# Spreading the sequence products to the end of attention, and loading the operands of the output projection ahead of their use

## The chip, the cores and the metric

The kernel runs on one core of a Trainium2 chip. The metric is the device time of one execution in microseconds (us). Engines are named as in the profile: PE is TensorE (its weight loads PEld), DVE VectorE, ACT ScalarE, POOL GpSimd, and SP the engine whose queue issues nearly all DMAs.

## What is computed

```python
x = A_x                                                     # [1, 2048, 512]
g = sigmoid((x * gate_w).sum(-1, keepdims=True))
# part A: real part of a 2-d DFT, as products with cos and sin matrices
a = dft_seq_re @ (x @ dft_hid_re.T) - dft_seq_im @ (x @ dft_hid_im.T)
# part B: causal attention in a window of 256 keys, 32 heads of 16
q, k, v = split(x @ wqkv)
p = softmax(where(0 <= i - j < 256, q @ k.T / 4, -1e9))
b = (p @ v) @ wo
return g * a + (1 - g) * b
```

All tensors are float32. Products that need it are split into a high and a low part (hi, lo), and three products replace one.

## The kernel before

**Two kinds of work on TensorE.** The attention runs in a main loop written out over n, and all other products ("dense" ones) come from one generator, `dense()`, from which `fill(n)` takes a number of steps per turn of the loop. A step is one product of hi and lo parts; in the loop it is written as two matmuls of 64 rows each. `fill` is called twice for each of the four turns p of a block n, and adds `rate / 2` to a quota each time; each whole quota is one step. The order of instructions on each engine is that in which this Python code issues them. A small clock (`tick`) counts steps, and `defer(ticks, fn)` puts a later instruction at the place where the clock has gone on by so many ticks. So `defer` sets places in the lists of the engines, not times.

**Attention.** 128 blocks (8 groups of 4 heads by 16 blocks of 128 rows). The S products of block n (`s_head`, L417) give row maxima by a fused step on DVE (L420). Four blocks of maxima are negated, split (L427, L428), transposed (L430), written to `m_scr` by DMA and read back into two rows of the tile `ring0`, as mask rows of the T products. Nine blocks later (`LAG`) the T products of block k = n - 9 (`t_head`, L472) are made, ACT takes their exponential (L473) into a tile `pt`, and POOL masks two parts of it (`t_mask`, L479 and L483). After every four blocks P V follows (`pv`, L498), 48 matmuls; ACT copies one half (L504), DVE adds the other (L505), and the result goes to DRAM (`u_scr`) and is repacked by DMA into `o_scr` (the values) and `l_scr` (the sums). The sums are read, inverted on DVE (L527) and written back.

The last nine turns of the loop have no S any more: these are the T blocks 119 to 127, with three P V between and behind them.

**Sequence products.** After the projections ("proj"), `c_block` makes 16 blocks of the DFT along the sequence, 24 steps each (L246). Each is evicted by ACT and DVE (L749 to L756), mixed into its rows (L765 to L774) and stored in `r_scr[tb]`. The last pair of blocks, 13 and 3, is mixed together, after the second of them. In this stage `rate` is the constant `FILL_SEQ = 2.3`. When the last block has been issued, "seq" is set.

**Output projection.** For each quarter `sb` of the rows and each of four groups g, `o_load` loads the broadcast inverse sums (`rl`) and the values (`o`), DVE multiplies them (L854), ACT casts the product to its high part in two pieces (L102), and DVE makes the low part in two (L105). The operands of quarter 0 are prepared as soon as its sums are there, those of 1 and 2 not before "seq", those of 3 after attention. Then `wo_run` makes tile tb = 0 to 15 with 12 products each (L242), and DVE adds the gated product to the mixed row read back from `r_scr` (L893), which is stored in `out`. Before tile 0 the first three mixed rows are read into the tile `fin`, which lies where `ring0` was.

The lines that the change touches are `FILL_SEQ` and `fill`, the count in `c_block`, `attention_done`, `o_load`, `wo_get`, `wo_run`, and the loop.

Of the kernel before, what the change touches and what calls it, by code (L numbers as in the profile page):

```python
# [18 lines left out]
D = 512  # L19
# [7 lines left out]
SCALE = 0.25  # L27
LAG = 9
NPT = 7
FILL_FIRST, FILL_PROJ, FILL_SEQ = 4.0, 1.55, 2.3  # L30
TERMS = ((0, 0), (0, 1), (1, 0))
HALVES = slice(0, 512), slice(512, 1024)
H = D // 2 + 1
# [18 lines left out]
def fnet_window_mix(ctx: ExitStack, tc: tile.TileContext, xT, x, wqk, wv, wm, wx, cc, wo, gw, out):  # L52
    nc = tc.nc
# [18 lines left out]
    r_scr = [dram.tile([P, D], F32, name=f"r_scr{c}") for c in range(16)]  # L72
# [22 lines left out]
    def ld(dst, src):  # L95
        nc.sync.dma_start(dst, src)  # L96

    def f(ap):
        return ap.bitcast(F32)

    def hi_of(hi, raw):
        nc.scalar.copy(hi, raw)  # L102

    def lo_of(lo, raw, hi, pool=False):
        (nc.gpsimd if pool else nc.vector).tensor_sub(lo, raw, f(hi))  # L105
# [6 lines left out]
    def split_raw(raw, at_=0, step=0, pool=0):  # L112
        t = st.tile([P, 2, 1024], F32R, name="hl")
        hi, lo = t[:, 0], t[:, 1]
        for n, c in enumerate(HALVES):
            for m, (fn, *args) in enumerate(((hi_of, hi[:, c], raw[:, c]), (lo_of, lo[:, c], raw[:, c], hi[:, c], pool > n))):
                if step:
                    defer(at_ + step * (n + 2 * m), fn, *args)
                else:
                    fn(*args)  # L120
        return hi, lo

    def big_tile():
        return big.tile([P, 2, U_W], F32R, name="big")
# [42 lines left out]
    for dk in range(DK):  # L167
        c = slice(dk * 256, dk * 256 + 256)
# [11 lines left out]
    for dk in (1, 2, 3, 0):  # L180
        if dk:
            first_w(dk)
        t = XT[dk, 0]
# [65 lines left out]
    def es_tile():  # L249
        return ev.tile([P, U_W], F32, name="es", bufs=3)  # L250
# [377 lines left out]
        nc.vector.tensor_scalar(flag, gl[0:1, 10:11], 0.0, None, op0=OP.is_le)  # L628

    order = CLEAR + [tb for p in PAIRED for tb in p]  # L630
    MRAW = {}
    MHL = {}

    def main_load(n):
        if n < len(order):
            tb = order[n]
            MRAW[n] = st.tile([P, 1024], F32, name="raw", bufs=3)
            b = MAINS[tb % 4]
            ld(MRAW[n].rearrange("p (q x) -> p q x", q=4),
               cc[tb][:, :, b:b + 2].rearrange("q p i t -> p q (i t)"))  # L640

    def main_split(n, at_=1, step=4):
        if n < len(order):
            MHL[n] = split_raw(MRAW.pop(n), at_, step, 2)

    def c_block(n, done):
        tb = order[n]
        clear = tb % 2 == 0
        pss = acc()
        hl = MHL.pop(n)  # L650
        m = 0
        for i in range(2):
            u = slice(0, H + 1) if i == 0 else slice(H, D + 1) if clear else slice(H + 1, 2 * H + 2)
            o = slice(H - 1, D) if clear and i else slice(0, H + 1)
            for q in range(4):
                k = (2 * q + i) * P
                for x, y in TERMS:
                    mm([ps[:, o] for ps in pss], hl[x][:, k:k + P], U[tb % 4, q][:, y, u], m == 0, m == 23,
                       True)
                    m += 1  # L660
                    if m < 24:
                        yield
        if FIN:
            wo_run()
        done(tb, pss)
        main_split(n + 2)
        defer(10, main_load, n + 3)
        yield

    have = set()  # L670

    def dense():
# [147 lines left out]
    def attention_done():  # L820
        FIN.append(const.tile([P, 8, 512], F32, name="fin", tag="ring0"))
        RL.append(const.tile([P, 4, 2, 512], F32, name="rl", tag="ring1"))
        for tb in range(3):
            defer(1 + 6 * tb, wo_get, tb)

    def by_class(ap):
        return ap.rearrange("r (c p) -> r c p", c=4)

    def rows_of(ap):
        return ap.rearrange("r (p c) -> r c p", c=4)  # L830
# [10 lines left out]
    def o_load(sb, g):  # L841
        ls = l_scr[sb][g // 2]
        if sb == 3:
            t = pt_tile([P, 3, 512], F32R)
            o = f(t[:, 2])
        else:
            t = big_tile()[:, :, 0:512]
            o = f(t[:, 1])
        rl = RL[0][:, sb * 2 - 4 + g // 2, g % 2] if FIN and sb > 1 else es_tile()[:, 0:512]
        ld(rl, bass.AP(tensor=ls.tensor, offset=ls[1, g % 2 * 8].offset, ap=[[512, 8], [0, 16], [1, 512]]))  # L850
        ld(o, o_scr[sb][g])

        def product():
            nc.vector.tensor_mul(rl, o, rl)  # L854
            defer(4, high)

        def high():
            for c, p in TURNS:
                hi_of(by_class(t[:, 0])[:, c], rows_of(rl)[:, c, p])
            defer(4, low)  # L860

        def low():
            for c, p in TURNS:
                lo_of(by_class(t[:, 1])[:, c], rows_of(rl)[:, c, p], by_class(t[:, 0])[:, c])
            defer(8, OHL[sb].append, t)
        defer(16, product)

    def wo_get(tb):
        if tb in stored and tb not in wo_r:
            wo_r[tb] = FIN[0][:, tb % 8]  # L870
            ld(wo_r[tb], r_scr[tb])

    def wo_run():
        nonlocal wo_next
        tb = wo_next
        sb, c = divmod(tb, 4)
        if tb > 15 or len(OHL.get(sb, ())) < NG or len(WO) < 4:
            return tick()
        wo_get(tb)
        if tb not in wo_r:  # L880
            return tick()
        wo_next += 1
        r = wo_r.pop(tb)
        w = 256 if tb == 15 else 512
        for q in range(0, 512, w):
            k = slice(q, q + w)
            ps = ps_a.tile([P, 512], F32, name="t", tag="st")
            n = 0
# [4 lines left out]
            nc.vector.scalar_tensor_tensor(r[:, k], ps[:, :w], g0[:, tb:tb + 1], r[:, k], op0=OP.mult, op1=OP.add)  # L893
            defer(3 if tb == 15 else 8, ld, out[sb][:, c, k], r[:, k])
        wo_get(tb + 3)

    stream = dense()
# [9 lines left out]
    def ring_ahead(n):  # L907
        nonlocal loaded
        while loaded < 4 * NS:
            g, ss = divmod(loaded, 4)  # L910
            if n >= NB * g + 4 * ss:
                need(("qk", g // 2, ss))
            if ("qk", g // 2, ss) not in have or n - LAG < NB * (g - 1) + 4 * ss + 5:
                break
            ring_load(g, ss)
            loaded += 1

    def fill(n):
        nonlocal quota
        rate = FILL_FIRST if n < LAG else FILL_SEQ if "proj" in have else FILL_PROJ  # L920
        quota += rate / 2
        while quota >= 1:
            next(stream, None)
            quota -= 1

    N = NS * NB
# [10 lines left out]

    for n in range(N + LAG + 1):
        k = n - LAG
        ring_ahead(n + 1)  # L940
        if k in (-2, 0):
            v_ahead(k // 2 + 1)
        for p in range(NH):
            if 0 <= k < N > n:
                s_head(n, p)
                t_head(k, p ^ 1)
            elif p % 2 == 0:
                for j in range(p, p + 2):
# [158 lines left out]
```

## Time and profile before

| | us |
|---|---|
| median of three runs | 731.53 |
| lowest and highest | 730.19, 732.51 |
| profiled execution | 732.08 |
| its span | 730.2 |

| engine | busy us in the span |
|---|---|
| PE | 603.6 |
| DVE | 495.2 |
| POOL | 435.1 |
| ACT | 428.4 |

The mean granted clock of TensorE was 0.877 of full speed. A row of the timeline gives the start and duration in us, the engine, the line of the kernel, the operation, and out<-in by the program's names with partitions x elements. Rows of one group in a row are merged (x96). In brackets stands how long the engine sat idle before it, and who released it. "SPq" rows are issues of DMAs. In the chain of waits a row is the start, the duration, and the work that held up the end at that time. A row of a stage gives, for the time from A to B, the stage's length, the busy time of each engine with its number of instructions, the granted clock, the share of the DMA engines and GB/s. Numbers of lines in rows are those of the kernel before; in the changed kernel L854 is L857, and L893 is L896.

### The profile page before, as it was taken

How to read it: one execution, taken by the hardware profiler on the slowest of the kernel's cores; microseconds unless marked ns; L12 is line 12 of the kernel's file. 1: busy time of each engine (PE TensorE's matmuls, PEld its weight loads, DVE VectorE, ACT ScalarE, POOL GpSimd, SP SyncE). 2: the span in 40 equal slices, each digit the busy share in tenths (PEclk: the TensorE clock that was granted, in tenths of full speed). 3: DMA queues.
4: the chain of work that ended last, by engine and by line, in shares of the span. 5: the costliest groups of instructions: out<-in, count | busy, mean ns of one | idle time of the engine just before them, and what ended most of it. 6: DMA issues, size and time to landing. Idle time of an engine off the chain costs nothing. (4 is left out here: it accounts for less than half of the span.)

```text
span 730.2 us, 17617 instructions
## 1 busy us (share of the span) xinstructions
PE 603.6 (83%) x6222; PEld 450.6 (62%) x6222; DVE 495.2 (68%) x1419; ACT 428.4 (59%) x952; POOL 435.1 (60%) x521
## 2 busy tenths in 40 slices
PE   9999699899788898988868887769777799559885
PEld 6788466666454666665546566657666587437664
DVE  5278677787787788787766765675688677344561
ACT  6434578677556676665556767476667668652220
POOL 6012557676687766678584979988988746420000
PEclk9999889999999999889988897667779969858898
DMA  7777677787565778567586699856566743655883
GB/s 278 259 233 199 205 228 225 228 263 210 176 201 172 213 227 273 179 202 207 169 262 214 210 268 278 269 148 188 171 195 197 207 138 117 190 174 145 259 276 110
DMA packets 93605, 152.61 MB, mean 209 GB/s; under 512 B 33028, under 2 KB 42116, under 8 KB 93380
## 3 DMA queue, kind: packets, MB, share of 16 engines
q1 hardware_dynamic: 92068, 149.28, 66.9%
q10 hardware_dynamic: 1440, 2.10, 0.9%
q8 instruction: 53, 0.87, 0.6%
q14 instruction: 44, 0.36, 0.2%
HBM read 108.56 MB, written 47.24 MB: 213 GB/s over the span
## 5 line engine op out<-in xcount | busy, mean ns | idle before, releaser
L420 DVE CUSTOM_DVE_ANT_0 sm<-s,mask 128x384 bf16<-128x384 f32 (+2 forms) x512 | 270.3, 528 | 104.3 <-PE s L417 54.7
L473 ACT ACTIVATE pt<-t 128x384 f32<-128x384 f32 (+2 forms) x512 | 231.4, 474 | 101.1 <-PE t L472 77.8
L472 PE MATMUL t<-ring,ring 50*128 50x384 f32 (+2 forms) x512 | 218.3, 442 | 59.0 <-ACT pt L473 30.1
L246 PE MATMUL d<-big,hl 64*128 64x512 f32 (+2 forms) x1440 | 248.8, 384 | 0.5 <-DVE es L257 0.5
L417 PE MATMUL s<-ring,ring 48*128 48x384 f32 (+2 forms) x512 | 199.0, 400 | 33.0 <-DVE nm L420 28.7
L246 PEld LDWEIGHTS d<-big,hl 64*128 64x128 f32 x1440 | 177.0, 223 | 6.5 <-issue 1.7
L417 PEld LDWEIGHTS s<-ring,ring 48*128 48x128 f32 x512 | 106.2, 212 | 99.6 <-DVE nm L420 86.7
L479 POOL TENSOR_SCALAR_AFFINE_SELECT pt<-pt 128x512 f32<-128x512 f32 x128 | 83.0, 649 | 140.5 <-ACT pt L473 140.0
L472 PEld LDWEIGHTS t<-ring,ring 50*128 50x128 f32 x512 | 108.1, 214 | 91.3 <-ACT pt L473 46.4
L246 PE MATMUL d<-hl,big 64*128 64x512 f32 x600 | 111.7, 416 | 0.0
L498 PE MATMUL o<-pt,vpad 64*32 64x320 f32 (+5 forms) x2816 | 89.2, 392 | 15.9 <-POOL pt L479 10.8
L498 PEld LDWEIGHTS o<-pt,vpad 64*32 64x32 f32 x2816 | 69.1, 117 | 38.4 <-POOL pt L479 13.6
L339 POOL TENSOR_TENSOR cv<-cv 128x256 f32<-128x256 f32 (+1 forms) x64 | 74.4, 1163 | 20.4 <-DMA cv<-cc 16.9
L483 POOL TENSOR_SCALAR_AFFINE_SELECT pt<-pt 128x512 f32<-128x512 f32 x112 | 74.8, 667 | 0.0
L246 PEld LDWEIGHTS d<-hl,big 64*128 64x128 f32 x600 | 67.1, 195 | 4.8 <-issue 1.0
L504 ACT COPY es<-o 128x512 f32<-128x512 f32 x32 | 18.8, 586 | 82.0 <-PE o L498 77.9
L342 POOL TENSOR_TENSOR cv<-cv 128x512 f32<-128x512 f32 x48 | 62.9, 1311 | 0.0
L540 ACT ACTIVATE cv<-cv 128x768 f32<-128x768 f32 x72 | 60.6, 842 | 0.6 <-POOL cv L339 0.6
L505 DVE TENSOR_TENSOR es<-o,es 128x512 f32<-128x512 f32 x32 | 22.0, 688 | 43.2 <-ACT es L504 35.9
L105 POOL TENSOR_TENSOR hl<-es,hl 128x512 fp32r<-128x512 f32 x14 | 18.5, 1319 | 48.0 <-ACT hl L102 48.0
L105 POOL TENSOR_TENSOR hl<-raw,hl 128x512 fp32r<-128x512 f32 x35 | 45.4, 1309 | 2.2 <-ACT hl L102 2.2
L242 PE MATMUL t<-big 128*128 128x512 f32 x144 | 40.0, 438 | 8.1 <-DVE fin L893 8.1
(98 smaller groups left out, 648.3 us busy)
## 6 DMA issues: line engine op xcount, KB each, us to landing
cv<-cc SPq DMA_DIRECT2D x64, 512.0 KB
qk_scr<-hl SPq DMA_DIRECT2D x32, 512.0 KB
ring<-qk_scr SPq DMA_DIRECT2D x128, 128.0 KB
ring<-qk_scr SPq DMA_DIRECT2D x128, 64.0 KB
u_scr<-es SPq DMA_DIRECT2D x32, 256.0 KB
raw<-cc SPq DMA_DIRECT2D x16, 512.0 KB
fin<-r_scr SPq DMA_DIRECT2D x17, 256.0 KB
big<-c_scr SPq DMA_DIRECT2D x16, 258.0 KB
```

The source lines that it names most:

```text
L105: (nc.gpsimd if pool else nc.vector).tensor_sub(lo, raw, f(hi))
L246: nc.tensor.matmul(pss[h], w[r], x[r], start=start, stop=stop, skip_group_check=skip)
L339: (nc.gpsimd if pool else nc.vector).tensor_sub(out, a, b)
L342: (nc.gpsimd if pool else nc.vector).tensor_add(out, a, b)
L417: nc.tensor.matmul(ps[:, :w], ring[0][r, p, jb * P:(jb + 1) * P], ring[1][r, p, k0:k0 + w], start=True, stop=True)
L420: nc.vector.tensor_tensor_reduce(out=sm[:, :w], in0=ps[:, :w], in1=mask[:, WIN - w:], scale=1.0, scalar=3e38, op0=OP.add, op1=OP.min, accu ...
L472: nc.tensor.matmul(ps[:, :w], ring[1][r, p, q0:q0 + P], ring[0][r, p, q0:q0 + w], start=True, stop=True)
L473: nc.scalar.activation(pt[:, j, :w], ps[:, :w], AF.Exp, scale=-1.0)
L479: nc.gpsimd.affine_select(a, a, pattern=[[0, 4], [1, P]], compare_op=OP.is_ge, fill=0.0, base=0, channel_multiplier=-1)
L483: nc.gpsimd.affine_select(a, a, pattern=[[0, 4], [-1, P]], compare_op=OP.is_gt, fill=0.0, base=0, channel_multiplier=1)
L498: nc.tensor.matmul(ot[h][32 * j:32 * j + 32, a - sb * 512:e - sb * 512], v2[r, j], pt[r, j, a - kb * P:e - kb * P], start=kb == kbs[0], st ...
L540: nc.scalar.activation(junk, src, AF.Abs, accum_out=dst)
```

## The change

1. In the stage of sequence products the rate is no longer a constant: it is reckoned at each call so that 48 steps (`SEQ_END`, two blocks) are left when S ends (n = N), and these are spread over the nine turns that have T blocks alone. For this `c_block` counts the steps that are left.
2. In `o_load` the inverse sums of quarters 0 to 2 are loaded into the half of the `big` tile where the high part will stand, instead of into an `es` tile (there are three of those) or the tile `rl`; the product goes to an `es` tile. The product stands 24 ticks behind the loads instead of 16, but for the last quarter.
3. The first three mixed rows are read into the tiles T[0] to T[2], which are free by then, from n = N + 4 on, where they are stored. All other mixed rows are read by DMAs that ACT issues instead of SP.
4. A result is stored 13 ticks after its sum instead of 8 (but for the last), and the masks of a T block without S are placed 1 tick after it instead of 3.

```diff
-FILL_FIRST, FILL_PROJ, FILL_SEQ = 4.0, 1.55, 2.3
+FILL_FIRST, FILL_PROJ, SEQ_END = 4.0, 1.55, 48
...
+                    left[0] -= 1
...
-            defer(1 + 6 * tb, wo_get, tb)
+            wo_get(tb)
...
-        rl = RL[0][:, sb * 2 - 4 + g // 2, g % 2] if FIN and sb > 1 else es_tile()[:, 0:512]
+        rl = RL[0][:, g // 2, g % 2] if sb == 3 else f(t[:, 0])
...
         def product():
-            nc.vector.tensor_mul(rl, o, rl)
-            defer(4, high)
+            to = rl if sb == 3 else es_tile()[:, 0:512]
+            nc.vector.tensor_mul(to, o, rl)
+            defer(4, high, to)
...
-        defer(16, product)
+        defer(16 if sb == 3 else 24, product)
...
         if tb in stored and tb not in wo_r:
-            wo_r[tb] = FIN[0][:, tb % 8]
-            ld(wo_r[tb], r_scr[tb])
+            wo_r[tb] = T[tb][:, 0:D] if tb < 3 else FIN[0][:, tb % 8]
+            (ld if tb < 3 else nc.scalar.dma_start)(wo_r[tb], r_scr[tb])
...
-            defer(3 if tb == 15 else 8, ld, out[sb][:, c, k], r[:, k])
+            defer(3 if tb == 15 else 13, ld, out[sb][:, c, k], r[:, k])
...
-        rate = FILL_FIRST if n < LAG else FILL_SEQ if "proj" in have else FILL_PROJ
+        if n < LAG:
+            rate = FILL_FIRST
+        elif "proj" not in have:
+            rate = FILL_PROJ
+        elif n < N:
+            rate = max(0, left[0] - SEQ_END) / (4 * (N - n) - 2)
+        else:
+            rate = left[0] / (4 * (N + LAG - n) - 2) if n < N + LAG else 0
...
+        if n >= N + 4:
+            for tb in range(3):
+                wo_get(tb)
...
-                defer(3, t_mask, k)
+                defer(3 if n < N else 1, t_mask, k)
```

How this moves instructions is seen at three places. The first is ACT in the T blocks without S, from the first P V there (the first L504) on. Before:

```order
L504 COPY es<-o 128x512
L473 ACTIVATE pt<-t 128x384 x4
L102 CAST big<-es 128x384
L102 CAST big<-es 128x128
L473 ACTIVATE pt<-t 128x384 x2
L102 CAST big<-es 128x384
L102 CAST big<-es 128x128
L473 ACTIVATE pt<-t 128x384 x2
L749 ACTIVATE es<-d_9756 128x258
```

And in the changed kernel:

```order
L504 COPY es<-o 128x512
L473 ACTIVATE pt<-t 128x384 x10
L751 ACTIVATE es<-d_9677 128x258
L473 ACTIVATE pt<-t 128x384 x4
L775 ACTIVATE ev<-es,g_332 128x257
L776 ACTIVATE ev<-es,g_332 128x255
L473 ACTIVATE pt<-t 128x384 x2
L102 CAST big<-es 128x384
L102 CAST big<-es 128x128
L504 COPY es<-o 128x512
```

The first cast of an operand of the output projection (big<-es) stood behind four exponentials, and now stands behind sixteen, just ahead of the copy of the next P V. Before the third P V all eight operands of quarters 0 and 1 were cast, now those of quarter 0 alone.

The second place is SP in the same stage, from the write of the last mask rows (m_scr_162) to their read. Before:

```order
L96 DMA m_scr_162<-mt 4x32x32
L96 DMA u_scr_1_177<-es 128x512
L96 DMA es<-l_scr_0_166 128x1x512
L96 DMA big<-o_scr_182 128x512
L96 DMA vr<-v_scr_113 128x4x64
L96 DMA es<-l_scr_1_167 128x1x512
L96 DMA big<-o_scr_182 128x512
L96 DMA ring_309<-m_scr_162 2x2x384 x2
```

And in the changed kernel:

```order
L96 DMA m_scr_162<-mt 4x32x32
L96 DMA u_scr_1_177<-es 128x512
L96 DMA vr<-v_scr_113 128x4x64
L96 DMA l_scr_1_167<-lt 128x64
L96 DMA big<-l_scr_0_166 128x1x512
L96 DMA big<-o_scr_182 128x512
L96 DMA ring_309<-m_scr_162 2x2x384 x2
```

Between the two there were two pairs of loads of operands (a pair is l_scr and o_scr), and there is one now, with the write of the inverse sums (l_scr<-lt); the load of the sums' broadcast goes to `big` instead of `es`.

The third place is DVE in the output projection, from the sum of a mixed row to the first low parts that follow. Before, at tile 0:

```order
L893 SCALAR_TENSOR_TENSOR fin<-t,g_333,fin 128x512
L854 TENSOR_TENSOR es<-big,es 128x512
L105 TENSOR_TENSOR big<-es,big 128x384
L105 TENSOR_TENSOR big<-es,big 128x128
L854 TENSOR_TENSOR rl<-big,rl 128x512
L893 SCALAR_TENSOR_TENSOR fin<-t,g_333,fin 128x512
```

And in the changed kernel, from tile 1 to tile 3:

```order
L896 SCALAR_TENSOR_TENSOR t_270<-t,g_333,t_270 128x512
L896 SCALAR_TENSOR_TENSOR t_271<-t,g_333,t_271 128x512
L857 TENSOR_TENSOR es<-big 128x512 x2
L527 RECIPROCAL lt<-lt 128x64
L896 SCALAR_TENSOR_TENSOR fin<-t,g_333,fin 128x512
L105 TENSOR_TENSOR big<-es,big 128x384
L105 TENSOR_TENSOR big<-es,big 128x128
L105 TENSOR_TENSOR big<-es,big 128x384
L105 TENSOR_TENSOR big<-es,big 128x128
L857 TENSOR_TENSOR es<-big 128x512 x2
```

Before, the operands that were made beside the first tiles were those of quarter 2; now they are the first of quarters 1 and 2, by turns (x2), and the sum of tile 3 stands ahead of their first low parts. On PE the last step of the sequence products stands behind the third P V, right ahead of the first product of the output projection; before, the last twenty T products and two P V had no step between them.

More of the change, by code (lines that the diff above doesn't have):

```diff
@@ L630, in fnet_window_mix @@
     order = CLEAR + [tb for p in PAIRED for tb in p]
+    left = [16 * 24]
     MRAW = {}
@@ L853, in product, with high, low @@
         def product():
-            nc.vector.tensor_mul(rl, o, rl)
-            defer(4, high)
-        def high():
+            to = rl if sb == 3 else es_tile()[:, 0:512]
+            nc.vector.tensor_mul(to, o, rl)
+            defer(4, high, to)
+        def high(o):
             for c, p in TURNS:
-                hi_of(by_class(t[:, 0])[:, c], rows_of(rl)[:, c, p])
-            defer(4, low)
-        def low():
+                hi_of(by_class(t[:, 0])[:, c], rows_of(o)[:, c, p])
+            defer(4, low, o)
+        def low(o):
             for c, p in TURNS:
-                lo_of(by_class(t[:, 1])[:, c], rows_of(rl)[:, c, p], by_class(t[:, 0])[:, c])
+                lo_of(by_class(t[:, 1])[:, c], rows_of(o)[:, c, p], by_class(t[:, 0])[:, c])
             defer(8, OHL[sb].append, t)
-        defer(16, product)
+        defer(16 if sb == 3 else 24, product)
     def wo_get(tb):
         if tb in stored and tb not in wo_r:
-            wo_r[tb] = FIN[0][:, tb % 8]
-            ld(wo_r[tb], r_scr[tb])
+            wo_r[tb] = T[tb][:, 0:D] if tb < 3 else FIN[0][:, tb % 8]
+            (ld if tb < 3 else nc.scalar.dma_start)(wo_r[tb], r_scr[tb])
     def wo_run():
```

## The prediction

> **What bounds the kernel now.** I read first the busy time by stage. The span falls into four: up to 430 us the projections, to about 620 attention beside the sequence products, to 662 the T blocks without S, to 722 the output projection, and 8.2 us of closing.
>
> ```profile
> core 0: us, PE busy (x) PEld busy (x) DVE busy (x) ACT busy (x) POOL busy (x), PEclk, DMA share, GB/s
> 430.00:620.00 190.00, 155.03 (x1879) 126.33 (x1879) 133.75 (x375) 127.34 (x288) 154.62 (x182) 0.78 0.65 193
> 620.00:662.00 42.00, 26.11 (x394) 20.03 (x392) 18.13 (x33) 24.95 (x59) 13.36 (x21) 0.64 0.56 173
> 662.00:722.00 60.00, 51.37 (x204) 39.88 (x204) 28.53 (x47) 11.45 (x19) 0.00 (x0) 0.91 0.70 228
> 722.00:730.20 8.20, 0.00 (x0) 0.00 (x0) 0.00 (x1) 0.00 (x0) 0.00 (x0) 0.63 0.11 27
> ```
>
> In the third stage no engine is busy for two thirds of it: it waits. The chain of waits says for what, then ScalarE's timeline:
>
> ```profile
> 628.26 5.46 DMA big<-o_scr
> 633.81 0.70 DVE es L854
> ...
> 654.30 7.14 DMA big<-o_scr
> ```
>
> ```profile
> 618.39 4.31 ACT L473 ACTIVATE pt<-t 128x384 f32<-128x384 f32 x10
> 630.33 1.19 ACT L102 CAST big<-es 128x384 fp32r<-128x384 f32 x2 [2.16 <-DVE es L854]
> 634.53 1.19 ACT L102 CAST big<-es 128x384 fp32r<-128x384 f32 x2 [2.25 <-DVE es L854]
> 651.15 0.67 ACT L473 ACTIVATE pt<-t 128x256 f32<-128x256 f32 x2
> 655.28 1.19 ACT L102 CAST big<-es 128x384 fp32r<-128x384 f32 x2 [3.46 <-DVE es L854]
> 659.46 0.45 ACT L473 ACTIVATE pt<-t 128x128 f32<-128x128 f32 x2
> 663.38 0.59 ACT L504 COPY es<-o 128x512 f32<-128x512 f32 x1
> ```
>
> The exponentials (L473) stand in ScalarE's list behind the casts of the output operands, and each cast waits for a load of 5 to 7 us. TensorE shows the result:
>
> ```profile
> 619.45 0.34 PE L417 MATMUL s<-ring,ring 48*128 48x384 f32 x1
> 622.68 2.49 PE L498 MATMUL o<-pt,vpad 64*32 64x64 f32 x96
> 636.57 2.37 PE L472 MATMUL t<-ring,ring 50*128 50x384 f32 x6 [7.25 <-ACT pt L473]
> 642.81 4.89 PE L498 MATMUL o<-pt,vpad 64*32 64x64 f32 x96 [1.23 <-ACT pt L473]
> 661.92 11.74 PE L242 MATMUL t<-big 128*128 128x512 f32 x48
> 709.78 11.70 PE L242 MATMUL t<-big,pt 128*128 128x512 f32 x60
> ```
>
> **Steps moved out of the S stage.** 36 steps of the sequence products stand behind the last S before, 49 after: 13 move. In a packed slot, four matmuls (two steps) fill the time to the next S:
>
> ```profile
> 601.89 0.40 PE L246 MATMUL d<-big,hl 64*128 64x258 f32 x4
> 602.32 0.44 PE L417 MATMUL s<-ring,ring 48*128 48x384 f32 x1
> ```
>
> 0.43 us for two, so 13 are worth at most 2.8 us. Where a block waits for something else they are worth nothing; below zero there is no reason. The S stage waits often (TensorE 155 of 190 us), so I take the middle, 1.5: the S stage ends at 618.3 instead of 619.8 (the last S in the rows above).
>
> **The T stage.** The end of the first P V there (X) is 5.4 us after the last S before (619.8 to 625.17); the 8 steps fewer ahead of it are offset by two casts of sequence operands on ScalarE, so I keep 5.4. The first cast of an operand now stands behind sixteen exponentials instead of four, 12 x 0.43 = 5.2 us later at least, and its loads are issued behind the same P V as before; so ScalarE no longer waits for them. If that cover were gone, a load's 5 to 7 us would come back. What is late next is the mask row of the last three blocks: the T product of block 123 needs it. Its load stands on SP behind the store of P V's result, the reciprocals and the first operand pair:
>
> ```profile
> 614.07 0.32 SPq L96 DMA_DIRECT2D u_scr<-es  x1
> 616.19 0.55 SPq L96 DMA_DIRECT2D l_scr<-u_scr  x1
> 632.11 0.56 SPq L96 DMA_DIRECT2D ring<-m_scr  x2
> ```
>
> ```profile
> 626.45 0.69 DVE L505 TENSOR_TENSOR es<-o,es 128x512 f32<-128x512 f32 x1 [0.86 <-ACT es L504]
> 649.06 0.68 DVE L854 TENSOR_TENSOR es<-big,es 128x512 f32<-128x512 f32 x1
> 674.81 0.75 DVE L893 SCALAR_TENSOR_TENSOR fin<-t,g,fin 128x512 f32<-128x512 f32 x1 [4.43 <-DMA fin<-r_scr]
> 685.83 0.55 DVE L527 RECIPROCAL lt<-lt 128x64 f32<-128x64 f32 x1
> 686.30 1.04 DVE L105 TENSOR_TENSOR big<-rl,big 128x384 fp32r<-128x384 f32 x2
> 697.80 1.15 DVE L105 TENSOR_TENSOR pt<-rl,pt 128x384 fp32r<-128x384 f32 x2 [0.34 <-ACT pt L102]
> 721.52 0.48 DVE L893 SCALAR_TENSOR_TENSOR fin<-t,g,fin 128x256 f32<-128x256 f32 x1 [0.93 <-PE t L242]
> ```
>
> X plus 1.3 (the two evictions), 0.55 (L527) and five issues of about 0.45: issued at X+4.1. In before the same load was issued at 632.11 and its matmuls ran at 636.57, 4.4 us; so it lands at X+8.5, while eight exponentials of 0.43 and the eviction would have let TensorE on at X+4.3. I charge the 4.2 us of difference; the lower bound is 0.
>
> ```profile
> 639.18 0.51 ACT L773 ACTIVATE ev<-es,g 128x257 f32<-128x257 f32 x1
> ```
>
> From there ScalarE sets the pace: eight exponentials (3.4), the three copies of one sequence block (1.3, at up to 0.51 each as in this row), a cast (1.2), P V's copy (0.6); then four exponentials each of 0.43, 0.33 and 0.23 (4.0), three casts (3.6), and a mask and the last piece of P V (1.1): 15.2. P V takes 2.49 at full clock and 4.89 at half (the granted clock of this stage was 0.64); part of it lies beside ScalarE, so I add 1.3 of a possible 4.8. The T stage then is 5.4 + 8.5 + 16.5 = 30.4 us, where it was 42.1. The first output product stands at 618.3 + 30.4 = 648.7 (P), before at 661.92.
>
> The Trainium skill ("TensorE: Matmul & The Clock Gate", Part 1) says that the clock is halved after about one idle window of 3.4 us and given back after about as long a busy one. By it the stage would lose an estimated 1.7 us, not up to 4.8. The trace agrees on the loss (the gap of 7.25 us) but not on the return: P V at 642.81 was still slow.
>
> **The output projection.** Tiles 0 to 3 are 48 products of 0.245 (the row at 661.92): until P+11.8 nothing waits, as their operands lie under the T stage. In before the operands of tiles 4 to 7 were loaded by then. Now they wait for the last sequence block, hence are issued behind P V's end: evictions 1.3, its store 2.1 (614.07 to 616.19), three copies: P+5. The first lands about 4.5 later:
>
> ```profile
> 686.78 4.54 DMA rl<-l_scr
> ```
>
> P+10, then. VectorE has to make eight operands (tiles 4 to 11, two by two) at 0.69 for a product and up to 1.15 for a low part. In its list stands ahead of the first low part the sum of tile 3, whose mixed row comes from the very last sequence block: VectorE's own add behind tile 0 (P+4.5), two copies (P+5.5), a store that SP issues behind two operand pairs (P+8.5), landing near P+12, and a load of about 4.4 (the wait in the row at 674.81): P+16.3, with P+12 and P+20 as bounds. Behind it up to the last operand of tile 4: one sum 0.75, eight products 5.5, eight low parts 9.2: 15.5. Tile 4 is whole at P+31.8, twenty microseconds after TensorE ran dry. Then eleven and a bit tiles of 12 x 0.245, 32.8 (the 60 of the row at 709.78, 24 of them half as wide, bear the price out), and 2.0 for half clock after the wait (bounds 0 and 3.4): P+66.6. Last sum 0.5 and closing 8.2, as before: P+75.3.
>
> The rest costs nothing. Loads of mixed rows on ScalarE's queue instead of SP's: the first three lie under the T stage, the others behind all casts, and are needed only when VectorE has finished the operands. Later stores of results: only the last counts, and its delay is unchanged. The masks one tick earlier: GpSimd was busy 13 of 42 us. The Trainium skill ("DMA: Bandwidth & Descriptors", Issuing engines are not separate DMA queues) says that a second issuing engine only saves issue time; by it those loads bring nothing, which is what the sum has.
>
> **Sum.** 648.7 + 75.3 = 724.0 of span, against 730.2. The profiled execution took 732.08, 1.9 more than its span, and 0.55 more than the median of the three, 731.53; so 725.4 for the median.
>
> **The rivals.**
>
> *Operands in time.* If tile 3's row lands before P+12 and the mask row is no wait, P is 644.5 and the operands of tile 4 follow their loads (last issue P+16, 4.5 for landing, 2.3 to make): P+23, 8.8 earlier. 725.4 - 4.2 - 8.8 = 712.4. For it: a store is read back in 2.1 us when the queue is free. Against: the queue isn't.
>
> *The operands at their old pace: slower.* From 649.06 to 687.3 before, eight operands took 38.3 us, 4.8 each. At that pace from P+10 the seventh, which completes tile 4, comes at P+43.5, 11.7 later than forecast: 737. The point where it decides is P+37.9, 6.1 later than forecast; beyond it the change loses. For it: the same loads, now beside three more on another queue. Against: the old pace was partly set by SP waiting for free buffers, which the new places of the loads end.
>
> *Nothing won: VectorE held in the S stage.* The small step that makes the mask rows (L427) takes 0.162 us at best. Its groups are, over the whole run, for ten of them in the S stage (26.17 us of VectorE), and one alone; then GpSimd's longest:
>
> ```profile
> L427 DVE TENSOR_SCALAR mhl<-nm x33: 162/532/11735, 41.3 to 624.9; 128x16 fp32r<-128x16 f32 x33
> ```
>
> ```profile
> 430.00:620.00 190.00, 26.17 (x10) 0.78 0.65 193
> ```
>
> ```profile
> 534.57 6.90 DVE L427 TENSOR_SCALAR mhl<-nm 128x16 fp32r<-128x16 f32 x1
> ```
>
> ```profile
> L342 POOL TENSOR_TENSOR cv<-cv 128x512 f32<-128x512 f32 x48 | 62.9, 1311 | 0.0
> ```
>
> GpSimd is busy 154.62 of the 190 us there. The order of this stage shifts, so such holds fall anew, either way; one more long one takes the 6.1 us: 732. The Trainium skill ("SBUF — State Buffer", shared port pair) has the second of VectorE and GpSimd blocked until the first one's instruction ends; by it a hold is an estimated 1.3 us, GpSimd's longest, and this rival would be worth little. The row of 6.90 differs and decides.
>
> **How the numbers follow.** Forecast 0.46 (its own range 719 to 731), operands in time 0.22, VectorE held 0.18, old pace 0.14. A measurement here can tell about 0.3%, 2.2 us, from no change. Faster: 0.42 of the forecast, 0.22, and 0.03 of the held case: 0.67. Same: 0.04, 0.10 and 0.02 of the old pace: 0.16. Slower: 0.05 and 0.12: 0.17. The range 713 to 736 leaves out a part of the fastest and of the slowest case.
>
> **What would show it.** Right: no wait of a cast in the T stage of the changed kernel, the first L242 near 649, a wait of TensorE of some 15 to 20 us in all from its 49th product on, ended by VectorE's L105, and VectorE's sum of tile 3 waiting for a load ahead of it. Wrong: casts that still wait ahead of exponentials; a first L242 beyond 655; tile 4 whole before P+25 or after P+38; an S stage that ends 4 us away from 618.

## The result, and the profile after

The changed kernel takes 750.15 us (median of four; 747.33 to 751.39), where the kernel before took 731.72 beside it: 1.0249 of it, with a 95% interval of 1.0216 to 1.0282. It is slower, where 725.4 was forecast. Here and below a time is the median of all executions, while a ratio leaves out those in which the chip ran in a slower state, so the two need not agree to the last digit. The profiled execution has a span of 749.7 us against 730.2, 19.5 more. By stage (length, busy time of each engine, granted clock, share of the DMA engines, GB/s), after the change:

```profile
core 0: us, PE busy (x) PEld busy (x) DVE busy (x) ACT busy (x) POOL busy (x), PEclk, DMA share, GB/s
430.00:628.60 198.60, 153.65 (x1857) 122.17 (x1857) 138.84 (x377) 125.23 (x284) 157.02 (x183) 0.80 0.64 188
628.60:665.10 36.50, 27.24 (x425) 22.25 (x423) 11.62 (x25) 22.68 (x56) 14.85 (x22) 0.77 0.49 151
665.10:741.10 76.00, 51.41 (x206) 38.88 (x204) 34.11 (x57) 15.72 (x28) 0.00 (x0) 0.80 0.63 201
741.10:749.70 8.60, 0.00 (x0) 0.00 (x0) 0.06 (x1) 0.00 (x0) 0.00 (x0) 0.78 0.10 26
```

All three stages missed. The S stage ends at 628.6 instead of 619.8 (+8.8; -1.5 was forecast). The T stage takes 36.5 us where it took 42.1 (30.4 was forecast). The projection and the closing take 84.6 us where they took 68.3 (75.3 was forecast). Together: 8.8 - 5.6 + 16.3 = 19.5.

TensorE's timeline from the last S on (idle time before a row, and its releaser, in brackets):

```profile
628.18 0.44 PE L417 MATMUL s<-ring,ring 48*128 48x384 f32 x1
633.61 4.09 PE L498 MATMUL o<-pt,vpad 64*32 64x64 f32 x96 [1.13 <-ACT pt L473]
649.25 2.92 PE L498 MATMUL o<-pt,vpad 64*32 64x64 f32 x96
660.80 4.04 PE L498 MATMUL o<-pt,vpad 64*32 64x64 f32 x96 [0.20 <-ACT pt L473]
665.08 11.41 PE L242 MATMUL t<-big 128*128 128x512 f32 x48
681.99 1.22 PE L242 MATMUL t<-big 128*128 128x512 f32 x2 [5.50 <-ACT big L102]
690.21 0.80 PE L242 MATMUL t<-big 128*128 128x512 f32 x1 [7.00 <-DMA big<-o_scr]
702.62 0.80 PE L242 MATMUL t<-big 128*128 128x512 f32 x1 [4.54 <-DVE big L105]
707.57 21.84 PE L242 MATMUL t<-big 128*128 128x512 f32 x85 [0.86 <-DVE big L105]
```

The last P V ends at 664.84, and the first output product (P) starts at 665.08. Tiles 0 to 3 run through until P+11.4; then TensorE stands until 707.57, which is P+42.5, but for a few products of tile 4 that it makes as each operand comes. From there the rest runs without a gap, as forecast. So the loss of the last stage is one wait, for the operands of tile 4. VectorE's list over that wait:

```profile
677.36 0.69 DVE L857 TENSOR_TENSOR es<-big 128x512 f32<-128x512 f32 x1 [2.87 <-DMA big<-o_scr]
688.30 0.55 DVE L527 RECIPROCAL lt<-lt 128x64 f32<-128x64 f32 x1 [8.19 <-DMA lt<-l_scr]
688.77 0.65 DVE L896 SCALAR_TENSOR_TENSOR fin<-t,g,fin 128x512 f32<-128x512 f32 x1
689.34 2.15 DVE L105 TENSOR_TENSOR big<-es,big 128x384 fp32r<-128x384 f32 x4
701.12 0.69 DVE L857 TENSOR_TENSOR rl<-pt,rl 128x512 f32<-128x512 f32 x1 [4.63 <-DMA pt<-o_scr]
```

The first operand is multiplied at P+12.3, when its load has landed; P+10 was forecast for the landing. Its low part stands behind a reciprocal of quarter 3's sums, which waits 8.19 us for its load, and behind the sum of tile 3; it comes at P+24.3. Later the product of a quarter 3 operand waits another 4.63 ahead of low parts that tile 4 needs. The chain of waits names the loads behind this:

```profile
670.07 6.63 DMA big<-l_scr
677.40 7.02 DMA big<-o_scr
684.50 8.15 DMA big<-l_scr
693.37 7.66 DMA pt<-o_scr
```

One load of 256 KB takes 6.6 to 8.2 us here, where 4.5 was assumed; the chain of the kernel before, which the prediction shows, has loads of 5.46 and 7.14 us.

In the S stage the difference is a VectorE step that stands still. Block 101 takes 15.5 us after the change and 9.7 before. First VectorE, GpSimd and the next S product in the changed kernel, then the same place of the kernel before:

```profile
495.52 11.27 DVE L427 TENSOR_SCALAR mhl<-nm 128x16 fp32r<-128x16 f32 x1
505.48 1.28 POOL L105 TENSOR_TENSOR big<-big 128x516 fp32r<-128x516 f32 x1
509.06 0.64 POOL L479 TENSOR_SCALAR_AFFINE_SELECT pt<-pt 128x512 f32<-128x512 f32 x1 [2.30 <-ACT pt L473]
507.75 0.68 PE L417 MATMUL s<-ring,ring 48*128 48x384 f32 x1 [6.67 <-DVE nm L420]
```

```profile
494.16 0.26 DVE L427 TENSOR_SCALAR mhl<-nm 128x16 fp32r<-128x16 f32 x1
493.66 0.73 POOL L342 TENSOR_TENSOR ev<-es 128x255 f32<-128x255 f32 x1
```

L427, a step over 16 elements, ends at 506.79, and GpSimd's last instruction before its pause ends at 506.76. In the kernel before it had waited only for the end of one instruction (494.39). During the hold in the changed kernel VectorE makes no row maxima, and the S product behind it waits 6.67 us for one.

The kernel before has such holds too. Its ten steps L427 in this stage take 26.17 us, as the prediction shows, and after the change they take 3 us more (length of the stage, VectorE's time in them, granted clock, share of the DMA engines, GB/s):

```profile
430.00:628.60 198.60, 29.13 (x10) 0.80 0.64 188
```

So it is less their sum that changed than where they fall, by the length of the blocks: blocks 101, 105 and 109 take 40.6 us together after the change and 28.2 before, while block 97 takes 13.8 and 14.9. Some 2 of the 8.8 us are there already when block 89 begins (429.27 against 427.32).

### The profile page after: what moved, and what is told of

The parts are those of the page before. It is cut to its first block, busy times and chain, and to the rows that moved or that the text cites. A ratio compares the mean times of both kernels' runs of the same rounds, so it can differ in the third digit from the quotient of the medians.

```text
span 749.7 us, 17627 instructions
## 1 busy us (share of the span) xinstructions
PE 602.8 (80%) x6222; PEld 447.0 (60%) x6222; DVE 499.3 (67%) x1419; ACT 426.8 (57%) x952; POOL 435.6 (58%) x521
## 4 chain that ended last, share of the span: by engine, by line
PE 41%; DVE 16%; DMA 14%; ACT 11%; POOL 8%; issue 7%; SPq 3%; DVEq 0%; POOLq 0%; ACTq 0%
PE d L246 14%; PE o L498 8%; DVE sm L420 7%; DMA ring<-m_scr 6%; PE t L472 5%; PE t L242 5%; PE s L417 5%; PE d L242 4%; DVE mhl L427 4%; ACT pt L473 3%; ACT cv L540 3%; SPq L96 3%; DMA big<-l_scr 2%; DVE es L505 2%; ACT es L504 1%
## 5 line engine op out<-in xcount | busy, mean ns | idle before, releaser
L420 DVE CUSTOM_DVE_ANT_0 sm<-s,mask 128x384 bf16<-128x384 f32 (+2 forms) x512 | 270.9, 529 | 99.4 <-PE s L417 49.4
L417 PE MATMUL s<-ring,ring 48*128 48x384 f32 (+2 forms) x512 | 198.0, 397 | 36.6 <-DVE nm L420 32.3
L246 PEld LDWEIGHTS d<-big,hl 64*128 64x128 f32 x1440 | 175.2, 217 | 6.4 <-issue 1.9
L417 PEld LDWEIGHTS s<-ring,ring 48*128 48x128 f32 x512 | 103.8, 206 | 103.9 <-DVE nm L420 89.4
L472 PEld LDWEIGHTS t<-ring,ring 50*128 50x128 f32 x512 | 106.4, 210 | 94.1 <-ACT pt L473 37.0
L498 PE MATMUL o<-pt,vpad 64*32 64x320 f32 (+5 forms) x2816 | 91.3, 400 | 14.8 <-POOL pt L479 8.7
L498 PEld LDWEIGHTS o<-pt,vpad 64*32 64x32 f32 x2816 | 71.1, 120 | 38.5 <-POOL pt L479 10.9
L483 POOL TENSOR_SCALAR_AFFINE_SELECT pt<-pt 128x512 f32<-128x512 f32 x112 | 75.3, 672 | 0.0
L246 PEld LDWEIGHTS d<-hl,big 64*128 64x128 f32 x600 | 68.3, 196 | 4.0 <-issue 0.8
L504 ACT COPY es<-o 128x512 f32<-128x512 f32 x32 | 18.8, 588 | 87.7 <-PE o L498 87.7
L242 PEld LDWEIGHTS t<-big 128*128 128x128 f32 x144 | 29.1, 207 | 34.9 <-DVE big L105 14.9
```

The source lines that it names most:

```text
L242: nc.tensor.matmul(pss[0], w, x, start=start, stop=stop, skip_group_check=skip)
L246: nc.tensor.matmul(pss[h], w[r], x[r], start=start, stop=stop, skip_group_check=skip)
L417: nc.tensor.matmul(ps[:, :w], ring[0][r, p, jb * P:(jb + 1) * P], ring[1][r, p, k0:k0 + w], start=True, stop=True)
L420: nc.vector.tensor_tensor_reduce(out=sm[:, :w], in0=ps[:, :w], in1=mask[:, WIN - w:], scale=1.0, scalar=3e38, op0=OP.add, op1=OP.min, accu ...
L472: nc.tensor.matmul(ps[:, :w], ring[1][r, p, q0:q0 + P], ring[0][r, p, q0:q0 + w], start=True, stop=True)
L483: nc.gpsimd.affine_select(a, a, pattern=[[0, 4], [-1, P]], compare_op=OP.is_gt, fill=0.0, base=0, channel_multiplier=1)
```

## The experiments

Theories: **A**, the pace itself makes the loss in the projection, since operands of quarters 1 and 2 are released only by the last sequence block; **B**, the mixed rows read on ScalarE's queue hold its casts; **C**, the longer S stage is holds of VectorE's mask step while GpSimd works; **D**, these holds lie beside other waits. Ratios are to the kernel before on the same chip (733.5 to 735.4 us there), with their 95% intervals; the changed kernel was not run again on those chips, and its 1.0249 stands for it. Stage lengths are of the profiled execution of each kernel. The pace by itself, with the sums left in the three es tiles, was not run, so what follows shows the pace with part 2 in place.

### Which part makes the loss

e1 undoes part 3 and the later stores:

```diff
-            wo_r[tb] = T[tb][:, 0:D] if tb < 3 else FIN[0][:, tb % 8]
-            (ld if tb < 3 else nc.scalar.dma_start)(wo_r[tb], r_scr[tb])
+            wo_r[tb] = FIN[0][:, tb % 8]
+            ld(wo_r[tb], r_scr[tb])
...
-            defer(3 if tb == 15 else 13, ld, out[sb][:, c, k], r[:, k])
+            defer(3 if tb == 15 else 8, ld, out[sb][:, c, k], r[:, k])
...
```

> The kernel before with the new pace, the new places of the operands (parts 1 and 2) and the earlier mask; mixed rows and stores as before. Theory A (the pace itself makes the loss: operands of quarters 1 and 2 can't be loaded before the last sequence block): the loss stays, 745 to 752 us, tile 4 whole some 40 us behind the first output product. Rival B (the rows read on ScalarE's queue hold the casts, 10.85 us of ScalarE in the changed kernel): most of it is gone, 735 to 741 us.

755.92 us, 1.0274 (1.0193 to 1.0355), tile 4 whole at P+43.7. The loss stays; B doesn't carry it.

e2 undoes part 1:

```diff
-            rate = max(0, left[0] - SEQ_END) / (4 * (N - n) - 2)
...
+        rate = FILL_FIRST if n < LAG else FILL_SEQ if "proj" in have else FILL_PROJ
```

> The changed kernel with the constant rate of 2.3 steps back, parts 2 to 4 kept. Theory A: operands of quarters 0 to 2 are loaded in the last turns again, TensorE doesn't run dry behind tile 3, and the S stage ends near 620 us; the time is that of before or a little less, 726 to 733 us. Rival B: the rows on ScalarE's queue still cost, 740 us or more.

725.01 us, 0.9887 (0.9809 to 0.9964): faster than before. TensorE in its projection:

```profile
652.17 11.60 PE L242 MATMUL t<-big 128*128 128x512 f32 x48
663.97 3.06 PE L242 MATMUL t<-big 128*128 128x512 f32 x12 [0.20 <-DVE t L894]
676.01 3.03 PE L242 MATMUL t<-big 128*128 128x512 f32 x12 [2.35 <-DVE fin L894]
```

Tile 4 follows tile 3. From the first product to the last it takes 54.7 us, where the changed kernel takes 75.6 and the kernel before 59.6. The T stage takes 36.6 us, as in the changed kernel: the pace had brought it nothing. The profiled execution is the quickest of the four (716.84), but the products take 54.9 and 55.7 us in e8 and e12 as well, which have no pace either. A holds, and the whole loss comes with the pace.

e3 reads all mixed rows on SP's queue:

```diff
-            (ld if tb < 3 else nc.scalar.dma_start)(wo_r[tb], r_scr[tb])
+            ld(wo_r[tb], r_scr[tb])
```

> The changed kernel with all mixed rows read by SP's queue. Theory A: within 3 us of the changed kernel (747 to 753 us), tile 4 as late. Rival B: 10 us less, near 740 us, tile 4 whole about 32 us behind the first output product.

748.74 us, 1.0176 (1.0084 to 1.0269); tile 4 at P+43.6. In the changed kernel ScalarE's queue does stand still for such a load:

```profile
670.13 10.85 ACTq L874 DMA_DIRECT2D fin<-r_scr  x2
681.08 0.86 ACT L102 CAST big<-es 128x384 fp32r<-128x384 f32 x1 [10.47 <-DMA r_scr<-ev]
```

With the load on SP this wait is only moved: the operands behind it on that queue come later instead. The interval overlaps the changed kernel's, so B is worth nothing that can be told.

### The release of the operands

e6 loads quarter 1 whole before quarter 2:

```diff
-        if sb == 3 and not FIN or sb and "seq" not in have:
+        if sb == 3 and not FIN or sb and "seq" not in have or sb == 2 and ("ld", 1, 3) not in have:
```

> The changed kernel with the loads of quarter 2 behind those of quarter 1 instead of by turns. Theory A1 (tile 4 waits because its operands are loaded by turns with quarter 2's, seven operands before it is whole): tile 4 whole 28 to 33 us behind the first output product instead of 42, time 740 to 746 us. Rival E (the sum of all loads and VectorE's work sets the end): the wait moves to tile 8, time 747 to 752 us.

750.98 us, 1.0181 (1.0088 to 1.0275). Tile 4 was whole at P+34.4 instead of 42.5, and the projection's products took 70.4 us: 5 us less, of which the time shows nothing that can be told. A wait came back at tile 8 (1.58 us, from P+44.6). So the turns are a part of the wait, the smaller one.

```profile
672.64 11.39 PE L242 MATMUL t<-big 128*128 128x512 f32 x48
707.09 10.17 PE L242 MATMUL t<-big 128*128 128x512 f32 x37 [2.69 <-DVE big L105]
```

e7 releases quarter 1 one sequence block sooner; its tiles are free then:

```diff
-        if sb == 3 and not FIN or sb and "seq" not in have:
+        if sb == 3 and not FIN or sb and ("seq" if sb > 1 else "mod1") not in have:
...
+            if n == 14:
+                have.add("mod1")
```

> The changed kernel with quarter 1 released when the last but one sequence block has been issued (its tiles are free then) instead of the last. Theory A (the release of the operands by the last sequence block is the loss): tile 4 follows tile 3 without a long wait, what is left waits at tile 8; the first output product up to 5 us later for four more pairs of casts on ScalarE; 733 to 742 us. Rival E: nothing won, 747 to 752 us.

736.19 us, 1.0004 (0.9937 to 1.0071): the whole loss of the projection is gone (its products take 60.3 us), with the S stage as long as in the changed kernel (its end at 629.6).

```profile
666.67 19.77 PE L242 MATMUL t<-big 128*128 128x512 f32 x84
693.19 4.50 PE L242 MATMUL t<-big 128*128 128x512 f32 x12 [6.75 <-DVE fin L898]
```

84 products, seven tiles, run through. This shows A most directly: whether the release stands 24 steps sooner decides it. The edit also keeps quarter 1's loads clear of quarter 2's, which by e6 is worth some 5 of the 15 us.

e13 reads quarter 3's sums later, so that the reciprocal no longer stands ahead of quarter 1's low parts:

```diff
-            defer(d, l_in)
+            defer(d if sb < 3 or not hf else 60, l_in)
```

> The changed kernel with the sums of quarter 3 read back some 46 ticks later, so that their reciprocal (L527) and quarter 3's first product no longer stand ahead of quarter 1's low parts on VectorE. Theory J (VectorE, held 8.2 us by that reciprocal and 4.6 us by that product, makes tile 4 late): tile 4 whole 30 to 34 us behind the first output product instead of 42; part of it comes back at tile 12, 740 to 747 us. Rival K (the loads of quarters 1 and 2, 7 us each, set it): tile 4 at 39 us or later, 748 to 754 us.

744.91 us, 1.0128 (1.0043 to 1.0213); the last wait for tile 4 ends at 697.37, P+35.1. VectorE now stands for the mixed row of tile 3 instead:

```profile
685.35 0.75 DVE L896 SCALAR_TENSOR_TENSOR fin<-t,g,fin 128x512 f32<-128x512 f32 x1 [7.85 <-DMA fin<-r_scr]
```

That is P+23.1, hardly sooner than the reciprocal's P+23.2. What is won, 7 us, comes behind it: from that sum to tile 4 it takes 12.0 us instead of 18.8, as no quarter 3 operand stands between. Theory J was right in the sum and half right in the place: it is quarter 3's products, not its reciprocal, that cost the time.

### The S stage

e4 makes L427 on ScalarE:

```diff
-        nc.vector.tensor_scalar(hl[:, 0], m, -1.0, None, op0=OP.mult)
+        nc.scalar.activation(hl[:, 0], m, AF.Copy, scale=-1.0)
```

> The changed kernel with the negation of the maxima (L427) made by ScalarE. Theory C (the 8.8 us that the S stage got longer are holds of this VectorE step while GpSimd works, 29 us in ten steps): the S stage ends 5 to 10 us earlier, near 620 us, time 740 to 745 us. Rival D (the holds lie beside other waits; the S stage is longer for another reason, such as the order of the steps): the S stage ends at 626 to 630 us still, 747 to 752 us.

749.55 us, 1.0187 (1.0099 to 1.0275), S stage end 630.1: as D forecast, but the test missed its aim. The hold went to the next step, again to the end of GpSimd's run:

```profile
500.29 10.01 DVE L428 SCALAR_TENSOR_TENSOR mhl<-nm,mhl 128x16 fp32r<-128x16 f32 x1 [1.14 <-ACT mhl L427]
508.99 1.28 POOL L105 TENSOR_TENSOR big<-big 128x516 fp32r<-128x516 f32 x1
512.37 0.63 POOL L479 TENSOR_SCALAR_AFFINE_SELECT pt<-pt 128x512 f32<-128x512 f32 x1 [2.10 <-ACT pt L473]
```

e5 takes both steps off VectorE in that stage:

```diff
-        nc.vector.tensor_scalar(hl[:, 0], m, -1.0, None, op0=OP.mult)
-        nc.vector.scalar_tensor_tensor(hl[:, 1], m, -1.0, f(hl[:, 0]), op0=OP.mult, op1=OP.subtract)
...
+            nc.scalar.activation(neg, m, AF.Copy, scale=-1.0)
+            nc.scalar.activation(hl[:, 0], m, AF.Copy, scale=-1.0)
+            nc.gpsimd.tensor_sub(hl[:, 1], neg, f(hl[:, 0]))
...
+        defer(12 if 20 < u < 29 else 0, turn_rows)
```

> The changed kernel; in the stage of sequence products the maxima are negated by ScalarE, their low part is made by GpSimd, and VectorE's transpose stands 12 ticks later, so no step of two SBUF operands is left on VectorE there. The run before showed that with L427 on ScalarE its successor L428 was held instead, until GpSimd fell idle. Theory C (the holds lengthen the stage): block 101 takes about 10 us instead of 15.5, block 109 about 11 instead of 15, the S stage ends at 615 to 621 us, time 738 to 743 us. Rival D (the pace's order alone): both blocks as long as in the changed kernel, S stage end 626 to 630, 747 to 752 us.

744.31 us, 1.0132 (1.0058 to 1.0207), S stage end 617.8. Block 101 takes 6.2 us, block 109 11.6. The time gains less than the stage, as the T stage takes 39.2 us here instead of 36.5. GpSimd's own small step, and the transpose on VectorE behind it (line numbers of this kernel):

```profile
498.40 0.23 POOL L434 TENSOR_TENSOR mhl<-neg,mhl 128x16 fp32r<-128x16 f32 x1
498.67 0.21 DVE L439 STREAM_TRANSPOSE mt<-mhl 128x32 f32<-128x32 f32 x1 [3.07 <-POOL mhl L434]
```

e8 is e5's edit without the pace:

> The changed kernel with the constant rate back (run e2) and the low part of the mask rows on GpSimd. Theory C: the 29 us of holds in ten steps are gone, of which blocks 97 and 109 show some 8 us: the S stage ends at 607 to 612 us, time 715 to 721 us. Rival D (the holds lie beside other waits): as without it, 723 to 728 us.

724.41 us, 0.9842 (0.9769 to 0.9916): not to be told from e2. So C holds under the pace and D without it. All profiles together show this, by the time from the first S product of block 89, about where the sequence products begin, to the end of the last S product of the stage:

| | steps on VectorE | steps on ScalarE and GpSimd |
|---|---|---|
| constant rate | 187.0 to 192.5 us (3 kernels) | 190.4, 190.5 (2) |
| new pace | 196.3 to 205.3, mean 199.9 (9) | 188.7 to 192.8, mean 191.0 (4) |

e4, whose L428 was held, is counted on the left. Under the pace the two columns lie 8.8 us apart, without it no more than single executions scatter. The edit also moves the transpose, so the 8.8 us are those of the whole edit; that they are the holds' is read from blocks 101 and 109. Why holds of much the same sum cost nothing at the constant rate is open.

e10 is the changed kernel with e5's and e7's edits:

> The changed kernel, pace kept, with the low part on GpSimd (run e5, which took 0.9 % off) and quarter 1 released one block earlier (run e7, 1.8 to 2.4 % off). Theories A and C together: both gains add, S stage end near 618 us, projection near 60 us, time 727 to 732 us, 0.985 to 1.0 of the kernel before. If they take away the same wait: 735 us or more.

725.18 us, 0.9875 (0.9835 to 0.9916): both gains add. S stage end 623.4, products of the projection 58.3 us, seven tiles without a wait. With the pace kept, undoing the two causes takes away the loss and more.

```profile
659.99 19.73 PE L242 MATMUL t<-big 128*128 128x512 f32 x84
```

### The T stage

e9 reads the last mask rows back at once:

```diff
-            defer(12, read)
+            defer(12, read) if u < 29 else read()
```

> The changed kernel with the last mask rows read back at once behind their write, ahead of the store of P V's result on SP's queue. Theory F (the wait of 4.3 us for the mask rows is on the path of the T stage): no wait of a T product for them, the T stage 32 to 33 us instead of 36.5, time 744 to 748 us. Rival G (ScalarE's casts and VectorE's steps in the same stage come late anyway): the wait is gone and another takes its place, T stage 35 us or more, 748 to 752 us.

753.13 us, 1.0268 (1.0222 to 1.0314). No T product waits for the rows, and the T stage still takes 36.5 us: theory G. ScalarE shows what took their place:

```profile
650.33 1.18 ACT L102 CAST big<-es 128x384 fp32r<-128x384 f32 x2 [1.66 <-DVE es L857]
656.25 1.20 ACT L102 CAST big<-es 128x384 fp32r<-128x384 f32 x2 [3.96 <-DVE es L857]
```

Casts of quarter 0, which wait for VectorE's product, and so for its load, ahead of exponentials, as in the kernel before. e14 brings these loads forward too:

```diff
-        d = 14 if hf else 40
+        d = (6 if sb == 0 else 14) if hf else 40
```

> Run e9 (mask rows first) with the sums of quarter 0 read and inverted 6 ticks behind each other instead of 14, so that its operands are loaded behind one P V less. Theory L (the T stage ends with the casts of quarter 0, which wait for their loads): the T stage is 30 to 33 us instead of 36.5, time 744 to 748 us. Rival M (ScalarE's and TensorE's own work and the half clock set it): 35 us or more, 748 to 753 us.

The T stage shrinks to 28.5 us:

```profile
625.82 0.69 PE L417 MATMUL s<-ring,ring 48*128 48x384 f32 x1 [4.31 <-DVE nm L420]
655.06 11.39 PE L242 MATMUL t<-big 128*128 128x512 f32 x48
```

So L holds for the stage. The median of its executions, 750.80 us, 1.0222 (1.0158 to 1.0287), doesn't show the 8 us, though the profiled one took 740.97; where they went in the others stays open.

### Combinations

e11 is the kernel before with part 2 alone:

> The kernel before with part 2 alone (sums loaded into the big tile, product 24 ticks behind the loads). Theory H (the gain without the pace comes from the operands' casts, which no longer wait on ScalarE ahead of the exponentials): the T stage shrinks from 42 to 36 to 38 us and the projection from 60 to 55 to 57: 722 to 727 us, 0.985 to 0.993 of before. Rival I (the mixed rows in free tiles and the later stores carry it): 729 to 734 us, 0.995 to 1.005.

735.95 us, 1.0017 (0.9973 to 1.0061). The T stage shrinks to 38.7 us, but the projection's products take 63.0 instead of 59.6, with waits for VectorE's sums in fin. The ratio is as rival I has it: the gain of e2 needs parts 3 and 4 as well. With them these products take 54.7.

e12 joins e2, e5 and e9; e15 joins e10, e9 and e14; e16 adds e13's edit to e15.

> The changed kernel with the constant rate back, the low part on GpSimd, and the last mask rows read ahead of P V's store (runs e2, e5 and e9 together). Theory F: the T stage 32 to 33 us instead of 37, time 717 to 722 us, 0.975 to 0.983 of before. Rival G: as run e8, 722 to 726 us, 0.983 to 0.99.

> Run e10 (low part on GpSimd, quarter 1 one block earlier) with the mask rows first and quarter 0 sooner. Theory L: 5 us less than e10, 718 to 722 us, 0.978 to 0.984 of before. Rival M: as e10, 0.985 to 0.99.

> Run e15 with the sums of quarter 3 later as well. Theory J: the operands of tiles 8 to 11 come earlier on VectorE, 1 to 4 us less than e15. If quarter 3 is then late itself at tile 12: as e15 or up to 5 us more.

e12: 723.49 us, 0.9855 (0.9815 to 0.9895), no better than e8, with a T stage of 37.9 us (G). e15: 723.28 us, 0.984 (0.9792 to 0.9889): its T stage is 29.3 us, but the projection's products take 62.8 instead of 58.3, with the wait at tile 7 that e10 has (6.11) and a further one of 1.31 at tile 4, behind which 27 products take 8.47 us at a granted clock of 0.80. e16: 734.27 us, 1.001 (0.9967 to 1.0052): quarter 3 is late itself, TensorE waits at tile 12 (P+49 to 57), and it takes 11 us more than e15 where at most 5 were expected. The kernels faster than both kernels of this case are e2, e8, e10, e12 and e15, 1.1 to 1.6% below the kernel before; among them the intervals overlap.

## Why the prediction was wrong

The span came out 25.7 us above the 724.0 of the sum: 10.3 in the S stage, 6.1 in the T stage and 9.3 behind the first output product. A step failed in each.

**The output projection: the step that failed is the one that makes tile 4 whole at P+31.8; it was P+42.5.** The mechanism was the right one, TensorE dry behind tile 3 because the operands of tiles 4 to 7 are released by the last sequence block; e2 and e7 show it. Two of its terms were too small. The sum of tile 3, behind which VectorE's first low part stands, was put at P+16.3 (bounds P+12 and P+20) and ran at P+23.7. The store of its mixed row is issued at P+8.0, where P+8.5 was forecast:

```profile
673.03 0.86 SPq L96 DMA_DIRECT2D r_scr<-ev  x2
```

But ScalarE's queue, which waits for this store before it loads the row, goes on at P+15.9 (the row at 670.13), where P+12 was forecast, and in e13 the row is there at P+23.1. So store and load took 15 us where 7.8 were put. The reciprocal of quarter 3's sums, which the prediction left out of VectorE's list though the order shown for DVE has it, waits as long beside it. The second term is the work from that sum to tile 4: 15.5 us became 18.8, with products of quarter 3 and a wait of 4.63 for one of them in between, which the prediction left out too. Without them (e13) it is 12.0.

The point named as deciding, P+37.9, was passed. The rival "old pace" (P+43.5) came within a microsecond of the time of tile 4. That is partly luck: it counts 4.8 us for each operand from P+10 on, while here no low part of these operands is made before P+24.3, and e13 is 7 us faster with the same loads of quarters 1 and 2. Its reason "against", that the new places of the loads end the waits, did not help: the loads on the chain took 6.6 to 8.2 us. The 4.5 of the sum was the shortest load of operands on the chain of the kernel before, which has others of 5.46 to 7.26.

**The S stage: -1.5 forecast, +8.8 measured.** The step that failed is "below zero there is no reason", which leaves the holds out of the sum. The 13 steps moved out bought nothing that can be told: the table has 191.0 us with the pace and 190.4 and 190.5 without, once the holds are away. What came in place of the gain was the third rival, holds of VectorE that fall anew, with its price of one long hold (6.1) somewhat too small. It was given 18% as if it excluded the others; it came together with a late tile 4, and the sum of two rivals was never worked out.

**The T stage: 30.4 forecast, 36.5 measured.** The wait for the mask rows was there as forecast (4.2; measured 4.32, TensorE held until 645.34):

```profile
645.34 1.08 PE L472 MATMUL t<-ring,ring 50*128 50x384 f32 x2 [4.32 <-DMA ring<-m_scr]
656.89 0.96 PE L472 MATMUL t<-ring,ring 50*128 50x256 f32 x2 [2.11 <-ACT pt L473]
```

The first P V ended 9.1 us behind the last S, not 5.4: it started late (5.0 us behind the last S, 2.9 before) and took 4.09 us at a granted clock of 0.63, where it took 2.49 at 1.00. The rest, 19.7 us instead of 16.5, holds the second P V of 2.92 and the third of 4.04, and exponentials behind a cast. The step that failed is the claim that ScalarE would no longer wait for loads there: the pace moved casts behind exponentials, but one cast of quarter 0 still waited 1.49 us ahead of exponentials, and with the mask rows at hand two waited 1.66 and 3.96 (e9). With these loads brought forward as well the stage takes 28.5 us (e14). And it is as short without the pace (e2, 36.6), so the gain credited to the pace belonged to the other parts.

**Right:** the first loads issued at P+5; the run from tile 4 to the end (33.0 us, forecast 34.8); no cost of the rows on ScalarE's queue (e3). Not seen at all: parts 2 to 4 together shorten the projection by some 5 us when the operands are in time (e2 against the kernel before).

## What to carry to other kernels

Before work is spread to the end of a stage, list what its last piece releases: here the last 24 steps held back the operands of tiles 4 to 11, and the wait cost 16 us where the moved steps were thought to save 1.5. When a wait is costed, write down every instruction that stands ahead on the engine in question and when each one's own input lands; the products of other data that were left out here were worth 7 us (e13). Rivals that don't exclude each other need a joint case.

## What the runs showed of the hardware

A small VectorE step whose operands all lie in SBUF can stand still over many GpSimd instructions, not one: 11.27 us over twelve of them in the changed kernel, 10.01 in e4. It came free within 0.04 us of the end of a GpSimd instruction, in the longest cases of the last one before GpSimd paused; at other times it got in behind the first (0.26 us in the kernel before). What lets it in at one boundary and not at another is open. Row maxima (L420), which read PSUM, took at most 0.56 us beside a busy GpSimd in the S stage. Taking one of two such steps away hands the hold to the second (e4).

The Trainium skill ("SBUF — State Buffer", Terms, shared port pair) has the second engine blocked until the first one's instruction ends. By that a hold would be an estimated 1.3 us, the longest GpSimd instruction of this stage in the changed kernel; the holds of 10 and 11 us disagree. The Trainium skill ("SBUF — State Buffer", Who interferes with whom) also counts steps with two SBUF inputs among those that contend, and there e4's L428 agrees.
